# Retention recurrence with a Mish feed-forward block: mask tables and pad zeros made later, and a planner told the load times that were seen

## The chip, the core and the metric

The kernel runs on one core of a Trainium2 chip. The metric is the device time of one execution in microseconds (us). Times quoted as "the median" are medians over several executions of the same kernel. A profile records one execution; its span is a little shorter than the device time (227.4 us beside about 229 us here).

The engines are named as in the profile: PE is TensorE's matmul side, PEld its weight loads, DVE is VectorE, ACT is ScalarE, POOL is GpSimd, SP is SyncE. SPq is the instruction queue of SyncE, from which this kernel issues nearly all its DMA transfers.

## The reference, cut to what matters

```python
# B, H, S, D = 4, 8, 768, 64 ; x: 3072 x 512 ; w_in: 512 x 2048 ; w_out: 2048 x 512
gamma = 1.0 - 2.0 ** (-5.0 - np.arange(H))
state = 0
for t in range(S):
    state = gamma * state + k[:, :, t]^T v[:, :, t]        # one 64 x 64 state per batch and head
    y[:, :, t] = q[:, :, t] @ state / sqrt(D)
x = y.transpose(0, 2, 1, 3).reshape(B * S, H * D)
h = x @ w_in
g = h * tanh(softplus(h))                                  # Mish
return g @ w_out
```

## The kernel before

The recurrence is done in chunks of 128 tokens. Within a chunk the scores q k^T are masked and multiplied with v. Across chunks a state is carried, which is updated by a product k^T v (tile `u_ps`). Twelve groups of 256 tokens, g0 to g11, go through the recurrence, and the 256 output rows of each group then go through the up-projection (`h_ps`), Mish (`gt`) and the down-projection (`o_ps`). Groups 0, 1 and 2 turn their k and q on TensorE. From group 3 on, that is done by two DMA transposes (`kt`, `qt`).

The order of all instructions on all engines is fixed in advance by a small list scheduler. Each task has a modelled duration per engine, a priority and its dependencies. The planner plays the tasks through with these durations and then emits the instructions in the order of the planned starts. A duration given to the planner costs no time on the chip. It changes only the order of the queues.

```python
class Plan:
    LAT = {"PE": 0.25, "DVE": 0.1, "ACT": 0.1, "POOL": 0.12, "DMA": 2.0}
    ...
    def run(self):
        ...
        starts = {"PE": 0.9, "DVE": 0.7, "ACT": 0.7, "POOL": 0.5, "DMA": 1.3}
        ...
                d = got.eng[e]                       # the modelled duration
                order.append((now, seq, got.fn, e, d))
    ...
order, end = plan.run()
for start, seq, fn, e, d in order:                   # emitted in the planned order
    fn(e)
```

The loads of a group, the casts (copies into a 16-bit format) and products that wait for them, and the two transposes are these. Group g+1's loads are planned when its buffers come free, and all of these DMA instructions are in SyncE's one queue.

```python
# loads of group g: q in one piece, k and v in two chunks each, all issued by SyncE
loads[g, n, c] = add({"DMA": 1.4 if n == "q" else 1.18}, fn, dprio(), ...)

# k product of group g (fk), and v cast into the padded tile vpad (fv); GpSimd alone, k from group 3 on and v from group 2 on
kd = add(two(512 * n, g < DT), fk, pr, [loads[g, "k", c] for c in cs] + [tabs, open_t], ...)
vd = add(... {"POOL": 0.55 * n}, fv, pr, [loads[g, "v", c] for c in cs] + ..., ...)

def dma_transpose(g):                                # SyncE, g >= 3
    a = add({"DMA": 2.3}, fk, dprio(), [kdep[g, 0]], [], [grp[g]])     # kt, needs the k product
    b = add({"DMA": 2.3}, fq, dprio(), qdep[g], [], [grp[g]])          # qt, needs the q product

# the state update of one head pair, on TensorE: needs the k product and the v cast
def um(e):
    u = loc["u"] = psp.tile([P, len(us), P], FP32, tag="u_ps", name="u_ps")
    for i, c in enumerate(us):
        nc.tensor.matmul(u[:, i], G["k16"][:, c, hs(hp)], G["vp"][:, c * HP + hp, 0:3:2], ...)
u1 = add({"PE": mm * len(us)}, um, pr, [kdep[g, 0], vdep[g, 0]], [ub], [grp[g]])
```

The parts that the change takes hold of are the zeros of the query pads (`pq`), the eight mask tables, and the modelled durations of the loads:

```python
        def pq(e, i=i):
            ENG[e].memset(qpads[i][0:64, :, :, 1], 0.0)
            ENG[e].memset(qpads[i][64:128, :, :, 0], 0.0)
        ...
        a = add({"POOL": 2.0}, pq, (40, (i + 1) % 3))

    mks = []
    for h in range(H):
        def mk(e, h=h):
            ENG[e].tensor_scalar(
                msk[:, h], tri, float(gamma[h] ** (-C)), None, op0=ALU.mult)
        mks.append(add({"DVE": 0.35}, mk, (30,), [tabs]))
```

The masks are read from group 2 on only. Groups 0 and 1 (the "early" groups, GE = 2) use another form of the mask.

## Time and profile before

| what | value | view |
| --- | --- | --- |
| median of 3 runs | 228.63 us (228.51 to 229.49) | times |
| profiled span | 227.4 us | page |
| TensorE busy | 207.0 us, 91% | page, engine table |
| TensorE's first matmul | 9.00 us | timeline |
| TensorE idle from 9.00 to 52 us | 6.2 us | windows |
| group 2's first up-projection | 52.06 us | timeline |
| last w_out block cast begins (it waited for the landing) | 49.50 us | timeline |

These are the first lines of the page of before. The engine table gives busy time, share of the span and instruction count. The other two lines divide the span into 40 slices, each digit being tenths of busy time.

```profile
span 227.4 us, 4200 instructions
...
PE 207.0 (91%) x1688; PEld 148.3 (65%) x1688; DVE 103.4 (45%) x247; ACT 98.7 (43%) x177; POOL 71.4 (31%) x64
...
PE   0389879699999999999999899999999999999993
...
DMA  6999999999999999898999999931002011022212
```

The reader sees a TensorE that is nearly full from the ninth slice on, and a DMA that is busy until slice 26 (about 148 us) and then almost idle.

The start, from the timeline of before (start, duration, engine, line, operation, tiles, shapes; in brackets the idle time before it and what ended it):

```profile
5.24 1.04 POOL L361 TENSOR_TENSOR qpn_95<-raw_q,tab 128x512 f16<-128x512 f32 x1
5.40 2.95 DVE L283 TENSOR_SCALAR msk<-idtri 128x128 f32<-128x128 f16 x4 [3.29 <-DMA idtri<-rn_identtri]
...
8.27 0.67 DVE L361 TENSOR_TENSOR qpn_95<-raw_q,tab 128x512 f16<-128x512 f32 x1
...
9.00 1.03 PE L497 MATMUL tq<-idtri,qpn_95 128*128 128x128 f16 x8 [9.00 <-DVE qpn_95 L361]
```

Four mask products stand ahead of VectorE's half of the query product, so TensorE starts at 9.00 us.

The middle, from the windows view of before (window, its length, busy us and instruction count of PE, PEld, DVE, ACT and POOL, granted clock, DMA share, GB/s):

```profile
40.00:52.00 12.00, 9.84 (x76) 6.17 (x76) 5.81 (x12) 6.81 (x18) 4.91 (x5) 1.00 1.00 317
52.00:90.00 38.00, 38.00 (x332) 29.09 (x330) 21.65 (x56) 18.58 (x33) 19.90 (x14) 1.00 1.11 217
90.00:120.00 30.00, 29.29 (x277) 23.66 (x275) 17.31 (x49) 18.38 (x33) 15.11 (x12) 1.00 0.98 194
120.00:160.00 40.00, 39.10 (x347) 29.30 (x346) 23.69 (x61) 18.94 (x36) 16.95 (x12) 1.00 0.90 168
```

TensorE has no idle time from 52 to 90 us, 0.7 us from 90 to 120 and 0.9 us from 120 to 160. First SyncE's queue in before, from the timeline of that engine (an entry lasts while the queue is occupied with issuing, not until the data lands):

```profile
90.77 1.23 SPq L441 DMA_TRANSPOSE kt<-k_1024  x1
92.05 0.57 SPq L314 DMA_DIRECT2D raw_q<-in_q_dram  x1
92.68 2.03 SPq L322 DMA_DIRECT2D raw_k<-in_k_dram  x2
94.75 3.89 SPq L322 DMA_DIRECT2D raw_v<-in_v_dram  x2
98.82 2.00 SPq L446 DMA_TRANSPOSE qt<-q_1216  x1
102.09 1.23 SPq L441 DMA_TRANSPOSE kt<-k_1214  x1
```

Then GpSimd in the same stretch of before, the lines of the k product and the v cast:

```profile
88.84 1.90 POOL L386 TENSOR_TENSOR k_1024<-raw_k,tab 128x1024 f16<-128x1024 f32 x1 [1.43 <-PE s_ps L478]
90.68 1.04 POOL L201 CAST vpad_97<-raw_v 128x1024 f16<-128x1024 f32 x1
...
100.17 1.90 POOL L386 TENSOR_TENSOR k_1214<-raw_k,tab 128x1024 f16<-128x1024 f32 x1 [1.64 <-DMA raw_k<-in_k_dram]
102.10 1.04 POOL L201 CAST vpad_98<-raw_v 128x1024 f16<-128x1024 f32 x1
```

And the chain of work that ended last in before, in order of time (start, duration, what), cut to its waiting pieces:

```profile
93.33 6.67 DMA raw_k<-in_k_dram
...
100.17 1.86 POOL k_1214 L386
...
102.10 1.05 POOL vpad_98 L201
103.19 0.27 PE u_ps L672 x2
...
107.62 6.29 DMA raw_v<-in_v_dram
...
114.06 1.05 POOL vpad_99 L201
115.15 0.22 PE u_ps L672
...
125.39 1.05 POOL vpad_97 L201
126.47 0.27 PE u_ps L672 x2
```

There is a loop in these lines. The transpose of one group's k is issued 0.03 us after that group's k product ends (88.84 + 1.90 = 90.74). The loads of the next group stand behind it in the same queue. They are issued from 92.05 us on, and the k load lands about 100.0 us. The next k product then runs from 100.17 to 102.07, and its transpose is issued at 102.09. This period is 102.09 − 90.77 = 11.32 us (the four from 78.49 to 123.71 us last 10.3 to 12.3, 11.3 in the mean): 1.23 for issuing the transpose, 0.57 for q, 0.61 for the first half of k, 6.67 from the issue of the second half to its landing, 1.90 for the product, and 0.34 in small gaps. The v cast follows at once and takes 1.04 us, and TensorE's first state update of the group follows the cast by 0.05 us. At groups 8 and 9 TensorE had been idle for 0.48 and 0.90 us before it.

### The profile page before, as it was taken

What the parts mean: (1) busy time and instruction counts of PE and PEld (TensorE: products, weight loads), DVE (VectorE), ACT (ScalarE), POOL (GpSimd) and SP (SyncE); (2) the same over time, 40 slices, a digit from 0 to 9 for tenths busy, and PEclk for the clock granted to TensorE, in tenths of its full rate; (3) what the DMA queues carried; (4) which work ended last, traced back from release to release, by engine and by line L of the source; (5) the groups of instructions that cost most, each with busy time, mean ns of one, the idle gap of its engine ahead of it and who ended that gap; (6) DMA issues with size and microseconds to landing.
All of it is one profiled execution on the core that took longest, in us unless ns stands there. A gap on an engine that the chain in (4) does not pass through costs nothing.

```text
span 227.4 us, 4200 instructions
## 1 busy us (share of the span) xinstructions
PE 207.0 (91%) x1688; PEld 148.3 (65%) x1688; DVE 103.4 (45%) x247; ACT 98.7 (43%) x177; POOL 71.4 (31%) x64
## 2 busy tenths in 40 slices
PE   0389879699999999999999899999999999999993
PEld 0278768546857979797968668757857767444441
DVE  2978446362768472567643585747101011112221
ACT  2268666743424656566655636533613534100000
POOL 8770001518372727373636471720000000000000
PEclk9999999999999999999999999999999999999998
DMA  6999999999999999898999999931002011022212
GB/s 159 238 238 349 346 223 286 393 272 204 255 200 213 203 193 228 188 184 185 213 208 164 241 220 189 205 95 60 34 3 92 0 49 46 0 92 93 95 46 92
DMA packets 91572, 38.63 MB, mean 170 GB/s; under 512 B 69921, under 2 KB 86433, under 8 KB 91553
## 3 DMA queue, kind: packets, MB, share of 16 engines
q1 hardware_dynamic: 91264, 38.28, 74.9%
q8 instruction: 13, 0.21, 0.4%
q10 hardware_dynamic: 288, 0.09, 0.2%
q14 instruction: 7, 0.05, 0.1%
HBM read 27.35 MB, written 6.29 MB: 148 GB/s over the span
## 4 chain that ended last, share of the span: by engine, by line
PE 68%; DMA 18%; POOL 4%; DVE 3%; ACT 3%; issue 1%; SPq 1%; ACTq 0%; POOLq 0%
PE o_ps L758 33%; PE h_ps L736 25%; DMA wst<-in_moe_w_out_dram 6%; DMA wst<-in_moe_w_in_dram 4%; PE s_ps L478 3%; DMA raw_k<-in_k_dram 3%; PE y_ps L699 3%; DMA raw_v<-in_v_dram 3%; DMA idtri<-rn_identtri 2%; PE u_ps L672 1%; ACT win_90 L199 1%; PE y_ps L703 1%; PE tq L497 1%; DVE msk L283 1%; POOL vpad_97 L201 1%
## 5 line engine op out<-in xcount | busy, mean ns | idle before, releaser
L736 PE MATMUL h_ps<-xt,win_90 128*128 128x256 f16 x768 | 94.1, 273 | 2.0 <-ACT gt L741 2.0
L758 PE MATMUL o_ps<-wout_91,gt 128*128 128x512 f16 x384 | 90.4, 379 | 2.2 <-POOL wout_91 L201 1.9
L736 PEld LDWEIGHTS <-win_90 128*128 128x128 f16 x768 | 73.8, 98 | 14.7 <-issue 1.5
L741 ACT ACTIVATE gt<-h_ps 128x512 f16<-128x512 f32 x96 | 56.9, 597 | 58.2 <-PE h_ps L736 58.2
L758 PEld LDWEIGHTS <-gt 128*128 128x128 f16 x384 | 36.8, 98 | 37.9 <-issue 2.8
L769 DVE COPY osb<-o_ps 128x512 f32<-128x512 f32 x24 | 16.6, 691 | 58.5 <-PE o_ps L758 58.3
L649 DVE TENSOR_TENSOR am<-s_ps,msk 128x512 f16<-128x512 f32 x40 | 27.7, 692 | 32.1 <-PE s_ps L478 31.7
L199 ACT CAST xt<-y_ps 128x256 f16<-128x256 f32 x44 | 19.6, 446 | 21.6 <-PE y_ps L703 20.2
L201 POOL CAST vpad_99<-raw_v 128x1024 f16<-128x1024 f32 x4 | 4.2, 1038 | 20.3 <-DMA raw_v<-in_v_dram 20.3
L497 PE MATMUL tq<-idtri,qpn_95 128*128 128x128 f16 x16 | 2.1, 312 | 9.0 <-DVE qpn_95 L361 9.0
L478 PEld LDWEIGHTS <-kt 128*128 128x128 f16 x96 | 8.0, 99 | 2.6 <-issue 0.8
L497 PEld LDWEIGHTS <-qpn_95 128*128 128x128 f16 x16 | 1.7, 146 | 9.1 <-DVE qpn_95 L361 9.0
L699 PE MATMUL y_ps<-am,vpad_99 128*128 128x128 f16 x64 | 7.1, 219 | 0.0
L478 PE MATMUL s_ps<-qpad_92,kt 128*128 128x256 f16 x32 | 6.5, 288 | 0.4 <-ACT qpad_92 L199 0.4
L699 PEld LDWEIGHTS <-vpad_99 128*128 128x128 f16 x64 | 5.5, 98 | 1.7 <-DVE am L649 0.7
L683 DVE SCALAR_TENSOR_TENSOR st_1_101<-st_0_100,tab,u_ps 64x64 f16<-64x64 f16 x20 | 5.6, 279 | 2.2 <-PE u_ps L672 1.8
L478 PE MATMUL s_ps<-qpad_94,kt 128*128 128x256 f16 x32 | 6.1, 273 | 0.0
L478 PE MATMUL s_ps<-qpad_93,kt 128*128 128x256 f16 x32 | 6.1, 273 | 0.0
L536 DVE TENSOR_TENSOR am<-s_ps,idtri 128x512 f16<-128x512 f32 x8 | 5.5, 686 | 1.3 <-PE s_ps L478 1.3
L199 ACT CAST win_90<-wst 128x1024 f16<-128x1024 f32 x5 | 5.1, 1047 | 2.1 <-DMA wst<-in_moe_w_in_dram 2.1
L201 POOL CAST wout_91<-wst 128x1024 f16<-128x1024 f32 x4 | 4.2, 1042 | 5.6 <-DMA wst<-in_moe_w_out_dram 5.6
L683 DVE SCALAR_TENSOR_TENSOR st_2_102<-st_1_101,tab,u_ps 64x64 f16<-64x64 f16 x16 | 4.5, 280 | 3.1 <-PE u_ps L672 2.8
(164 smaller groups left out, 218.2 us busy)
## 6 DMA issues: line engine op xcount, KB each, us to landing
raw_q<-in_q_dram SPq DMA_DIRECT2D x12, 512.0 KB, 4.9
raw_k<-in_k_dram SPq DMA_DIRECT2D x24, 256.0 KB, 5.6
raw_v<-in_v_dram SPq DMA_DIRECT2D x24, 256.0 KB, 5.2
out_dram<-osb SPq DMA_DIRECT2D x24, 256.0 KB, 2.0
wst<-in_moe_w_in_dram SPq DMA_DIRECT2D x8, 512.0 KB, 7.6
wst<-in_moe_w_out_dram SPq DMA_DIRECT2D x8, 512.0 KB, 7.8
idtri<-rn_identtri ACTq DMA_DIRECT2D x1, 64.0 KB, 4.2
tab<-rn_tab ACTq DMA_DIRECT2D x1, 22.0 KB, 2.5
```

Source lines behind the costliest of these rows:

```text
L199: nc.scalar.copy(dst, src)
L201: ENG[e].tensor_copy(dst, src)
L478: nc.tensor.matmul(t, G["kt"][:, c, hp], G["qp"][:, :, hp, :, c * (C // 2):(c + 1) * (C // 2)].rearrange("p e y i -> p y e i"), start=True ...
L497: nc.tensor.transpose(t[:, e2, x, hh], G["qn"][:, e2 * HP + 2 * j + x, hh:hh + 2], ident)
L536: nc.vector.tensor_tensor(am, loc["s"].rearrange("p x y i -> p (x y) i"), tri.unsqueeze(1).broadcast_to((P, 4, C)), op=ALU.mult)
L649: nc.vector.tensor_tensor(am, loc["s"], msk[:, hs(hp)].unsqueeze(1).broadcast_to((P, CG, 2, C)), op=ALU.mult)
L683: nc.vector.scalar_tensor_tensor(tn[o, o], prev[o, o], tab[o, GC + hp:GC + hp + 1], loc["u"][o, i, o], op0=ALU.mult, op1=ALU.add)
L699: nc.tensor.matmul(y[:, c], G["vp"][:, c * HP + hp, hh:hh + 2], loc["am"][:, c, hh], start=(hh == 0), stop=(st is None and hh == 1))
L736: nc.tensor.matmul(h[:, j], win16[:, bp, fb * P:(fb + 1) * P], xtt[i][:, bp], start=(bp == 0), stop=(bp == NBP - 1))
L741: nc.scalar.activation(gtt[i][:, 2 * a:2 * a + 2], loc["h"], AF.Mish, scale=inv_boost)
L758: nc.tensor.matmul(ott[i, t], gtt[i][:, fb, t * P:(t + 1) * P], wout16[:, fb], start=(fb == 0), stop=(fb == NFB - 1))
L769: nc.vector.tensor_copy(osb, ott[i, t])
```

## The change

The intent was, by its description, to make the mask tables and the zeros of the late query pads once the first group is through, and to set the load model of the planner to the rates that had been seen. The diff, with comments and two neutral lines cut:

```diff
-    LAT = {"PE": 0.25, "DVE": 0.1, "ACT": 0.1, "POOL": 0.12, "DMA": 2.0}
+    LAT = {"PE": 0.25, "DVE": 0.1, "ACT": 0.1, "POOL": 0.12, "DMA": 1.5}
...
-        for d in deps:
+        for d in filter(None, deps):
...
-        starts = {"PE": 0.9, "DVE": 0.7, "ACT": 0.7, "POOL": 0.5, "DMA": 1.3}
+        starts = {"PE": 0.9, "DVE": 0.7, "ACT": 0.7, "POOL": 0.5, "DMA": 2.5}
...
-    tabs = add({"ACT": 1.6}, lambda e: None, (0,), [c_tab])
+    tabs = add({"ACT": 3.2}, lambda e: None, (0,), [c_tab])
...
-        a = add({"POOL": 2.0}, pq, (40, (i + 1) % 3))
+        a = None if i < GE else add({"POOL": 2.0}, pq, (40,))
...
-    mks = []
-    for h in range(H):
-        def mk(e, h=h):
-            ENG[e].tensor_scalar(
-                msk[:, h], tri, float(gamma[h] ** (-C)), None, op0=ALU.mult)
-        mks.append(add({"DVE": 0.35}, mk, (30,), [tabs]))
...
-            loads[g, n, c] = add({"DMA": 1.4 if n == "q" else 1.18}, fn, dprio(), [],
+            loads[g, n, c] = add({"DMA": 1.5 if n == "q" else 1.2}, fn, dprio(), [],
...
-        ld = add({"DMA": 1.3}, fn, dprio(), [], [wbuf[kind, j]])
+        ld = add({"DMA": 1.5 if kind == "in" else 1.3}, fn, dprio(), [], [wbuf[kind, j]])
...
             if g == GE - 1:
+                for h in range(H):
+                    def mk(e, h=h):
+                        if e == "ACT":
+                            nc.scalar.mul(msk[:, h], tri, float(gamma[h] ** (-C)))
+                        else:
+                            nc.vector.tensor_scalar(
+                                msk[:, h], tri, float(gamma[h] ** (-C)), None,
+                                op0=ALU.mult)
+                    mks.append(add({"DVE": 0.35, "ACT": 0.3}, mk, (17,), xdone[0]))
```

So the change has three parts: the masks move from the head of VectorE's queue to a later place on VectorE or ScalarE; the zeros of two of the three query pads, four memsets on GpSimd, go away (the early groups write these pads whole); and six constants of the planner change, which may reorder every queue and hand a task to another engine.

More of the change, by code (lines that the diff above doesn't have):

```diff
@@ L427, in load_w @@
                             [ld], [], [wbuf[kind, j]])
+    mks = []
     state = [None] * HP
```

## The prediction

> **What bounds the kernel now.** TensorE: the engine table gives it 207.0 of 227.4 us. Its 20.4 us of idleness, from the windows view, are 9.0 us before its first matmul, 6.2 between 9 and 52 us, 1.6 between 90 and 160, and 3.6 of tail. After 52 us matmuls run nearly back to back, so the time is set by when that dense stretch begins, plus later holes.
>
> Start: the first transposes wait 9.0 us for the second half of the query product on VectorE. That half begins at 8.27, behind four mask products that held VectorE from 5.40 to 8.35 (the timeline). The first took 1.85 us, the shortest 0.22.
>
> Then the load queue. By the windows it moves about 217 GB/s for the k and v loads (256-byte rows), 349 for w_in and 390 for w_out, without a break from 3 to 49 us. The last w_out block lands at about 49.5 us; the first up-projection of group 2, where the dense stretch begins, is at 52.06.
>
> **What the change does.** By the instruction order, the eight mask products leave the start of VectorE's queue (four go to ScalarE; four later on VectorE). Four memsets of query pads, 0.94 to 0.98 us each, leave GpSimd; it takes a k product, v casts and three w_in casts. Load order up to the last w_out block is unchanged; TensorE has the same instructions in another order.
>
> **Costs.** The query product's halves can start when raw_q lands, about 5.2 us. The Trainium skill, "SBUF — State Buffer", "SBUF: two separate sides", says that a VectorE operation with two SBUF inputs and a GpSimd operation reading SBUF exclude each other; the 1.85 us mask beside GpSimd's product (5.24 to 6.28) agrees. So I serialize the halves: 5.2 + 1.04 + 0.67 = 6.9 us. TensorE starts 2.1 us earlier (1.8 to 2.7).
>
> Little of that is on the path that ends last. Work before 52 us needs loads: group 1's last v at 16.8, w_in until 30.1, w_out until 49.5, and these stay. The skill, "DMA: Bandwidth & Descriptors", "Specifications", puts the line-rate limit at 512-byte transfers; the rates above agree, and no transfer grows. TensorE will idle more between its start and 52 us: about 7.3 us for 6.2. The order of down-projection parts does help: before, six down matmuls and four y groups stood between the last w_out cast and group 2's up-projection; now only two. That cast moves to GpSimd (1.04 instead of 0.69 us): 49.5 + 1.04 + 0.5 = 51.1 us, a gain of 1.0. Later holes may change by 0.5 us.
>
> **Prediction:** 227.4 us, 80% range 225.6 to 229.0. Faster by over 2%: 0.04; within 2%: 0.92; slower by over 2%: 0.04.
>
> **What would show it.** Right: first matmul near 6.9; last w_out block within 1 us of 49.5; group 2's first up-projection near 51; idleness between TensorE's start and 52 us grows, on w_out and w_in casts. Wrong: that landing moves earlier by over 2 us (late casts had starved the queue); or holes after 52 us change by over 1.5 us, since an output store now precedes a v load, and a k transpose a q transpose, in SyncE's queue.
>
> **What would make it wrong.** A queue that fills better once GpSimd casts w_in at once (dip to 165 to 189 GB/s at 32 to 34 us): up to 1.5 us more gain. A new stall in the in-order queues: up to 2 us lost.

## The result and the profile after

Four executions of the changed kernel had a median of 226.45 us (225.60 to 226.99), beside 228.68 us (228.51 to 229.49) for four of the kernel before. The ratio is 0.9892, with a 95% interval of 0.9853 to 0.9931. A gain of 1.1% is "the same" at the 2% mark, and 226.45 lies in the predicted range. It is about 1 us under the central value.

The profiled run was the slowest of the four, 226.99 us, with a span of 225.2 us. Its granted clock fell to 0.76 between 13 and 20 us, and the mean for the whole run was 0.989.

The first lines of the page of after:

```profile
span 225.2 us, 4187 instructions
...
PE 209.0 (93%) x1688; PEld 149.1 (66%) x1688; DVE 103.0 (46%) x249; ACT 95.4 (42%) x174; POOL 68.9 (31%) x61
...
PE   0868999999998999999999999999999999999993
```

TensorE is busy for 8 tenths of the second slice, where it was busy for 3 before, but the next two slices have 6 and 8 tenths, where they had 8 and 9. Its work is the same 1688 matmuls.

The start, from the timeline of after:

```profile
5.22 0.69 DVE L355 TENSOR_TENSOR qpn_95<-raw_q,tab 128x512 f16<-128x512 f32 x1 [3.10 <-DMA raw_q<-in_q_dram]
5.26 1.55 POOL L355 TENSOR_TENSOR qpn_95<-raw_q,tab 128x512 f16<-128x512 f32 x1
5.97 0.60 PE L493 MATMUL tq<-idtri,qpn_95 128*128 128x128 f16 x4 [5.97 <-DVE qpn_95 L355]
...
6.87 0.60 PE L493 MATMUL tq<-idtri,qpn_95 128*128 128x128 f16 x4 [0.29 <-POOL qpn_95 L355]
```

TensorE now starts at 5.97 us, because four of the first eight transposes need only VectorE's half of the query product. GpSimd's half took 1.55 us here, against 1.04 us before when it ran beside a mask product. That agrees with the Trainium skill, "SBUF — State Buffer", "SBUF: two separate sides", where a VectorE operation with two SBUF inputs and a GpSimd operation that reads SBUF hold the shared ports in turn: the GpSimd operation began last and took 0.51 us longer, which fits a standstill for most of the 0.65 us that the two overlapped.

The middle, from the windows view of after:

```profile
40.00:52.00 12.00, 11.28 (x82) 6.26 (x80) 6.90 (x17) 5.99 (x12) 4.99 (x4) 1.00 1.11 330
52.00:90.00 38.00, 37.06 (x312) 27.25 (x310) 22.56 (x58) 16.55 (x30) 15.91 (x11) 1.00 1.01 212
90.00:120.00 30.00, 29.49 (x283) 24.12 (x282) 17.85 (x50) 18.55 (x34) 14.30 (x10) 1.00 0.99 200
120.00:160.00 40.00, 39.62 (x362) 30.93 (x360) 23.57 (x61) 20.76 (x38) 17.65 (x12) 1.00 0.91 166
```

From 40 to 52 us TensorE is busier by 1.4 us. Then it loses 0.9 us between 52 and 90 us, where before lost none. From 90 to 160 us it loses 0.9 us instead of 1.6. So the early gain is partly given back at once, and that speaks against a plain reading of "starts earlier, ends earlier".

The chain that ended last in after, cut to its waiting pieces:

```profile
112.24 1.91 POOL k_1410 L380
...
114.17 1.23 SPq L437
...
119.78 4.91 DMA raw_v<-in_v_dram
...
124.83 1.05 POOL vpad_97 L201
...
131.38 6.36 DMA raw_v<-in_v_dram
...
137.88 1.05 POOL vpad_98 L201
...
138.97 0.27 PE u_ps L668 x2
```

The chain still runs through a k product, SyncE's queue, a load and a v cast, but in this run it meets TensorE at group 10 (138.97 us), not at group 9. Following group by group shows more than the chain does. Group 8's first state update waited too, until 116.09 us, while group 9's was ready 1.35 us before TensorE came to it.

### The profile page after: what moved, and what is told of

Read it like the earlier page. It is cut to its first block, busy times and chain, and to the rows that moved or that the text cites. A ratio compares the mean times of both kernels' runs of the same rounds, so it can differ in the third digit from the quotient of the medians.

```text
span 225.2 us, 4187 instructions
## 1 busy us (share of the span) xinstructions
PE 209.0 (93%) x1688; PEld 149.1 (66%) x1688; DVE 103.0 (46%) x249; ACT 95.4 (42%) x174; POOL 68.9 (31%) x61
## 4 chain that ended last, share of the span: by engine, by line
PE 67%; DMA 14%; SPq 10%; POOL 3%; DVE 2%; ACT 1%; issue 1%; POOLq 0%; DVEq 0%
PE o_ps L754 33%; PE h_ps L732 24%; SPq L316 7%; DMA raw_v<-in_v_dram 5%; DMA wst<-in_moe_w_out_dram 4%; DMA raw_k<-in_k_dram 3%; PE y_ps L695 3%; PE s_ps L474 3%; DMA raw_q<-in_q_dram 3%; PE u_ps L668 1%; SPq L308 1%; PE y_ps L699 1%; SPq L437 1%; POOL vpad_98 L201 1%; POOL k_1410 L380 1%
## 5 line engine op out<-in xcount | busy, mean ns | idle before, releaser
L199 ACT CAST xt<-y_ps 128x256 f16<-128x256 f32 x42 | 18.7, 445 | 20.1 <-PE y_ps L699 15.2
L201 POOL CAST vpad_98<-raw_v 128x1024 f16<-128x1024 f32 (+1 forms) x5 | 4.3, 867 | 5.8 <-DMA raw_v<-in_v_dram 3.4
L679 DVE SCALAR_TENSOR_TENSOR st_1_101<-st_0_100,tab,u_ps 64x64 f16<-64x64 f16 x20 | 5.6, 278 | 0.7 <-PE u_ps L668 0.3
L201 POOL CAST wout_91<-wst 128x1024 f16<-128x1024 f32 x3 | 3.1, 1042 | 8.6 <-DMA wst<-in_moe_w_out_dram 8.6
L679 DVE SCALAR_TENSOR_TENSOR st_1_104<-st_0_103,tab,u_ps 64x64 f16<-64x64 f16 x20 | 5.6, 278 | 0.4
L679 DVE SCALAR_TENSOR_TENSOR st_2_102<-st_1_101,tab,u_ps 64x64 f16<-64x64 f16 x16 | 4.5, 280 | 2.5 <-PE u_ps L668 2.2
```

The costliest lines, as they stand in the source:

```text
L199: nc.scalar.copy(dst, src)
L201: ENG[e].tensor_copy(dst, src)
L679: nc.vector.scalar_tensor_tensor(tn[o, o], prev[o, o], tab[o, GC + hp:GC + hp + 1], loc["u"][o, i, o], op0=ALU.mult, op1=ALU.add)
```

## The theories

**Pace.** TensorE's queue is in order. Each group's first state update has a fixed amount of TensorE work queued ahead of it. If TensorE gets there before that group's v cast, it waits, and everything that was gained before is lost at that point. The end of the kernel is then the time of the last such v cast, plus the work still queued behind it, plus about 4 us of tail and small holes. The casts come at the pace of the loads, one group per 11.3 us or so. What the new planner constants do is put more feed-forward work ahead of each group's state update, so less is left behind.

**Rivals.** (a) The prediction's own: the time is set by when the dense stretch near 52 us begins, through the start, the last w_out block and the order of the down-projection parts. (b) The early start: masks and pads out of the way are the gain. (c) The mask tables on ScalarE and the missing memsets free the engines later on.

The amount of work ahead of a group's first state update was worked out from the built kernels: the order of TensorE's instructions, with durations read from the chain of before (8 up-projection matmuls 0.87 us, 4 down-projection matmuls 0.86, a 128x128 matmul 0.0545, a 128x256 score matmul 0.109). These are estimates of TensorE time in us. The whole work is 200.9 us (200.5 with the durations as rounded here). Counted again in the traces, every entry below agrees to 0.3 us. The columns are the kernels, including those of the experiments:

| group | before, masks and pads moved only | after, constants only | q, k, v constants only | faster loads modelled | slower loads modelled |
| --- | --- | --- | --- | --- | --- |
| g4 | 48.2 | 51.6 | 49.9 | 46.5 | 51.6 |
| g6 | 71.4 | 74.9 | 73.1 | 68.8 | 75.7 |
| g8 | 93.8 | 96.4 | 95.5 | 90.4 | 99.0 |
| g9 | 104.0 | 107.5 | 106.6 | 99.7 | 110.1 |
| g10 | 115.2 | 118.6 | 117.8 | 110.8 | 121.2 |

The theory can be checked on before: the last wait is at group 9, whose cast ended at 126.42 us. 126.47 + (200.9 − 104.0) + 4.0 = 227.4 us, the span. The 4.0 is the remainder here. If the theory holds, it must be about the same in every kernel, whichever group is the last pinned one. It is: 4.1 in e1 (group 8), 3.9 in e4 (group 10), 4.0 in e10 (group 9), 4.0 in e11 (group 10) and 4.3 in e12 (group 4), each worked out in the same way from the two tables of this document.

## The experiments

Twelve kernels were run, all correct, each in five rounds beside the kernel before on the same chip. "Pinned" means that a group's first state update began 0.05 us after its v cast ended, so that the cast released it. The wait can be too short to show: the profile has no idle time of TensorE at the last pinned product of e6 and of e11.

| run | median us | before | ratio (95%) | span | first matmul | last pinned group: product begins, left behind it |
| --- | --- | --- | --- | --- | --- | --- |
| e1_after_again | 226.68 | 229.32 | 0.9900 (0.9866 to 0.9935) | 224.6 | 6.13 | g8: 116.03, 108.60 |
| e2_masks_late | 229.31 | 229.32 | 1.0007 (0.9975 to 1.0040) | 227.4 | 5.88 | g9: 126.53, 100.90 |
| e3_late_wst7 | 228.97 | 229.32 | 0.9994 (0.9964 to 1.0024) | 228.4 | 6.07 | g9: 127.49, 100.90 |
| e4_masks_head | 226.48 | 229.32 | 0.9888 (0.9859 to 0.9917) | 224.8 | 7.49 | g10: 138.60, 86.24 |
| e5_model_only | 226.19 | 228.87 | 0.9871 (0.9833 to 0.9910) | 224.2 | 6.38 | g8: 115.61, 108.60 |
| e6_masks_pads_only | 228.41 | 228.87 | 0.9982 (0.9941 to 1.0022) | 226.4 | 5.96 | g9: 125.48, 100.90 |
| e7_order_by_hand | 229.91 | 228.87 | 1.0037 (0.9993 to 1.0080) | 228.4 | 9.15 | g9: 127.50, 100.92 |
| e8_order_by_hand_masks_late | 229.34 | 228.87 | 1.0007 (0.9964 to 1.0050) | 227.4 | 5.90 | g9: 126.53, 100.91 |
| e9_plan_start_lat | 227.82 | 229.43 | 0.9932 (0.9909 to 0.9955) | 225.5 | 6.37 | g9: 124.63, 100.92 |
| e10_plan_qkv | 226.87 | 229.43 | 0.9908 (0.9873 to 0.9942) | 225.1 | 9.03 | g9: 126.83, 98.30 |
| e11_plan_fast | 232.08 | 229.43 | 1.0124 (1.0100 to 1.0147) | 230.2 | 8.33 | g10: 136.14, 94.07 |
| e12_after_slow | 225.10 | 229.43 | 0.9824 (0.9796 to 0.9851) | 223.9 | 6.01 | g4: 70.33, 153.57 |

### e1_after_again: the changed kernel once more

No edit. It ran on another chip, to have the change measured in the rounds of e2 to e4.

> The changed kernel, unaltered, as the yardstick of the runs beside it. Expected 225.6 to 227.0 us; last w_out block lands near 48.2 us, group 2's first up-projection begins near 49.8, as in its first profile.

Measured: 0.9900, so the gain is real and repeats. The profile of this run shows the last wait at group 8. From the timeline of e1, TensorE:

```profile
116.03 0.22 PE L668 MATMUL u_ps<-vpad,k 128*128 128x128 f16 x1 [0.74 <-POOL vpad L201]
```

Group 8's cast came 0.9 us later than in before (115.98 instead of 115.10). Only 108.60 us were left behind the product instead of 112.24, of which 2.6 (96.4 − 93.8) is work that now stands ahead, 0.9 is the hole at group 9, which is gone, and 0.1 is not accounted for. 0.9 − 3.64 is the whole difference of spans, −2.8 us.

### e2_masks_late: the early start alone

The order of before on every engine, except that the eight mask products are issued just ahead of VectorE's product of q for group 2. Nothing else moves, because the planner still plans them at the old place.

```diff
-    mks = []
+    mks, late = [], []
     for h in range(H):
         def mk(e, h=h):
-            ENG[e].tensor_scalar(
-                msk[:, h], tri, float(gamma[h] ** (-C)), None, op0=ALU.mult)
+            late.append(h)
...
             def fq(e):
+                while late:
+                    h = late.pop(0)
+                    nc.vector.tensor_scalar(
+                        msk[:, h], tri, float(gamma[h] ** (-C)), None, op0=ALU.mult)
                 ENG[e].tensor_tensor(
```

> The kernel before, every instruction in its old order, but the eight mask products issued just before VectorE's query product of group 2 instead of at the head of its queue. TensorE should start at 6.0 to 6.9 us. Theory LOADS (the dense stretch begins when the last w_out block is in; a start 3 us earlier is spent waiting): that block lands within 0.7 us of 49.5, group 2's first up-projection begins within 0.9 us of 52.06, and the time is 227.5 to 228.6. Rival START (the earlier start carries through): dense stretch 2 to 3 us earlier, time 225.7 to 226.7.

Measured: TensorE starts at 5.88 us, 3.1 us sooner, and the time is the same (1.0007). Rival (b) falls. The timelines of e2, first GpSimd, then TensorE, at group 9:

```profile
125.44 1.04 POOL L201 CAST vpad<-raw_v 128x1024 f16<-128x1024 f32 x1 [1.43 <-DMA raw_v<-in_v_dram]
```

```profile
126.53 0.27 PE L675 MATMUL u_ps<-vpad,k 128*128 128x128 f16 x2 [1.36 <-POOL vpad L201]
```

The same product in the timeline of before, TensorE:

```profile
126.47 0.27 PE L672 MATMUL u_ps<-vpad_97,k_1591 128*128 128x128 f16 x2 [0.90 <-POOL vpad_97 L201]
```

The wait at this product grew from 0.90 to 1.36 us. It starts at 126.53 instead of 126.47. A TensorE that comes earlier waits longer, and goes on at the same time. The line of GpSimd in e2 also corrects a reading of before: there, the profile puts the wait of this cast down to a TensorE instruction (y_ps at line 703). In before the v load had landed only at 125.24 us, 0.15 before the cast began (in e2 the two are 0.14 apart), so it was the load there too. The median, 229.31 us, lies over the written 227.5 to 228.6, but so does that of before in this call, 229.32; the ratio is what counts.

### e3_late_wst7: one more buffer for weights

As e2, and with seven staging buffers for weights instead of six, to let the load queue fill better. To make room, the mask tables are kept in half precision.

```diff
-    wst = ctx.enter_context(tc.tile_pool(name="rn_wst", bufs=6))
+    wst = ctx.enter_context(tc.tile_pool(name="rn_wst", bufs=7))
...
-    msk = cpool.tile([P, H, C], FP32)
+    msk = cpool.tile([P, H, C], FP16)
```

> As e2, with seven staging buffers for weight blocks instead of six (the mask table is held in 16 bits to make room); same order on every engine. Theory STARVED (part of what made w_out land earlier is that loads waited for a staging buffer less): SyncE no longer waits for the first w_in cast near 18 to 20.8 us, the last w_out block lands 0.8 to 1.5 us earlier than in e2, and the time falls by 0.5 to 1.3 us against e2. Rival SATURATED (the load queue was full all along): landing and time within 0.3 us of e2.

Measured: 0.9994, and the last w_out cast is at 48.78 us instead of 49.09 in e2, where the theory STARVED had written a landing 0.8 to 1.5 us earlier. The planner's own count of six slots was left as it was, so this tests the hardware's buffer and not a new order. A starved weight queue is not what bounds the kernel.

### e4_masks_head: the changed kernel with masks at the head again

As after, and four mask products are computed once more at the head of VectorE's queue, so that TensorE starts late. The order of all else is that of after.

```diff
+                    if e == "DVE" and g == 0:
+                        for h in range(4):
+                            nc.vector.tensor_scalar(
+                                msk[:, h], tri, float(gamma[h] ** (-C)), None,
+                                op0=ALU.mult)
                     ENG[e].tensor_tensor(
```

> The changed kernel, same order, with four of its mask products also computed at the head of VectorE's queue (they are computed again later, so results are unchanged). TensorE should start at about 9.0 us instead of 6.0. Theory LOADS: the last w_out block lands within 0.4 us of e1, group 2's first up-projection is at most 0.8 us later, and the time is at most 0.8 us over e1. Rival START: 2 to 3 us over e1.

Measured: TensorE starts at 7.49 us, not at the 9.0 that I had expected, since the four masks took 1.40 us together here. So the delay was 1.5 us instead of 3. It cost nothing: 0.9888 beside 0.9900 for e1. The last w_out block landed 0.56 us later than in e1 (at most 0.4 had been written) and group 2's first up-projection began 0.58 us later, which cost nothing either. Together with e2, the start is free of cost in both directions.

### e5_model_only and e6_masks_pads_only: the two halves of the change

e5 is before with only the planner's constants of the change. e6 is before with only the moved masks and the missing pad zeros, and the old constants. (The edits are the corresponding lines of the diff above.)

> The kernel before with only the planner's load constants of the change (masks and pad memsets stay where they were). Theory ORDER (the gain comes from the order in which the planner, given slower loads, queues the work: the first down-projection no longer stands ahead of up-projections and attention in TensorE's queue while its weights are still loading): 226.0 to 227.3 us, a ratio of 0.988 to 0.994, with no wait of TensorE on a w_out cast over 0.5 us. Rival UNLOADING (the gain comes from taking the masks and memsets off VectorE and GpSimd): 228 to 229.5, ratio 0.997 to 1.003.

> The kernel before with the masks and pad memsets moved as in the change, and the planner's old load constants. Theory ORDER: the 1.9 us wait of TensorE on the second w_out cast stays, ratio 0.996 to 1.002, although TensorE starts near 6 us. Rival UNLOADING: ratio 0.988 to 0.994.

Measured: 0.9871 for the constants alone, 0.9982 for the moved masks and pads (an interval that holds 1). The whole gain is that of the constants, which take no work off the chip. Rival (c) is ruled out as the cause. For rival (b) e5 alone would not do, since the new constants also put most of the masks behind the query product and TensorE starts at 6.38 us there. But e6 starts at 5.96 us without such a gain, and e10 below at 9.03 us with one.

Two details were missed. For e6 I had written that the wait of 1.9 us on the second w_out cast stays: it fell to 0.5 us, and group 2's first up-projection began at 50.68 us instead of 52.06, without a gain clear of noise. And e5 lies just under the written 0.988 to 0.994. The pins agree: e5 has the work ahead of after and ends 108.60 us after group 8's product, to the hundredth as e1; e6 has the work ahead of before and ends 100.90 us after group 9's product, as e2.

### e7_order_by_hand and e8_order_by_hand_masks_late: the order of the down-projection parts alone

This is the term that the prediction counted on. e7 is before, with only two blocks of TensorE's queue moved by hand, so that no down-projection should stand in the way of group 2's up-projection for a w_out block. e8 is e7 with the late masks of e2.

```diff
+            parts[i, t, part] = mmf
...
     order, end = plan.run()
+
+    def move(what, behind=None, before=None):
+        x = next(r for r in order if r[2] is parts[what])
+        order.remove(x)
+        n = next(n for n, r in enumerate(order) if r[2] is parts[behind or before])
+        order.insert(n + 1 if behind else n, x)
+    move((0, 0, 0), before=(0, 0, 1))
+    move((0, 1, 2), before=(0, 0, 3))
```

> The kernel before, with two moves by hand in TensorE's queue only, all other engines in their old order: the first four down matmuls go behind two blocks of up-projection (16 matmuls) and an attention unit, and the four that need no late weights (tile 1, part 2) go ahead of the eight-matmul tail that waits for the last w_out block. Theory ORDER: the wait of 1.9 us on the second w_out cast goes, group 2's first up-projection begins at 50.6 to 51.2 instead of 52.06, ratio 0.993 to 0.997. Rival LOADS ONLY (the last w_out landing sets the time, and only an earlier landing helps): ratio 0.998 to 1.002.

> As e7, with the mask products also moved away from the head of VectorE's queue, so that TensorE starts near 6 us. Theory ORDER with a bound from the last w_out block: at most 0.5 us better than e7, because the last w_out landing (about 49.3) plus cast and two matmuls is what is left. Rival START: 1.5 to 3 us better than e7, once the order no longer hides it.

Measured: 1.0037 and 1.0007. For e7 I had expected 0.993 to 0.997, and that was a miss. The wait of the down-projection for w_out on GpSimd, 1.9 us in before, is gone from the list of waits, but group 2's first up-projection began only at 51.72 us, not at the written 50.6 to 51.2. In place of that wait stands this line (from the waits of TensorE in e7: what waited for what, us in total, times, longest):

```profile
PE u_ps L672 <- POOL vpad L201: 2.8, 5, 1.1
```

The same waits in before:

```profile
PE u_ps L672 <- POOL vpad_97 L201: 1.1, 2, 0.9
PE u_ps L672 <- POOL vpad_99 L201: 0.5, 1, 0.5
```

A hole was closed and others opened downstream. They are not all due to an earlier TensorE: in the profile of e7, group 9's cast also ended 1.0 us later than in before (127.45 instead of 126.42), for a reason that stays open. In e8, where the up-projection began at 51.26 us, 0.8 us earlier than in before, the time is still that of before. (By the medians e8 is 0.57 us under e7, where at most 0.5 had been written; the intervals overlap.) Both speak against the prediction's view that the time is set near 52 us.

### e9, e10: which constants

e9 is before with only the start of the DMA (2.5), its latency (1.5) and the tables (3.2) of the change. e10 is before with only the load durations of q (1.5) and of k and v (1.2).

```diff
# e9
-    LAT = {..., "DMA": 2.0}
+    LAT = {..., "DMA": 1.5}
-        starts = {..., "DMA": 1.3}
+        starts = {..., "DMA": 2.5}
-    tabs = add({"ACT": 1.6}, ...)
+    tabs = add({"ACT": 3.2}, ...)
# e10
-            loads[g, n, c] = add({"DMA": 1.4 if n == "q" else 1.18}, ...
+            loads[g, n, c] = add({"DMA": 1.5 if n == "q" else 1.2}, ...
```

> The kernel before with three of the planner's new constants only: loads start at 2.5, landing latency 1.5, tables ready after 3.2. Theory PACE (TensorE reaches the first state-update product of a group at the pace of the v casts, which the load queue sets; the end is that moment plus the TensorE work queued behind it; the constants matter only where they change how much work is queued ahead of those products): the work ahead of groups 4 to 11 is exactly that of before (104.0 us ahead of group 9 by unit costs), so nothing changes: ratio 0.996 to 1.003; product of group 9 without slack after its cast, 100.9 us before the end. Rival ANY NEW ORDER (every re-planning with the new start or latency helps): 0.988 to 0.994.

> The kernel before with only the planner's durations of q, k and v loads raised (1.4 to 1.5 and 1.18 to 1.2). Theory PACE: 95.5 us of work stand ahead of group 8's product (before 93.8) and 106.6 ahead of group 9's (before 104.0); with casts done at 115.2 to 116 and 125.5 to 126.5 us the span is 224.5 to 225.7, a ratio of 0.988 to 0.994; group 9's product begins over 0.5 us after its cast. Rival: the gain needs the w_in constant or the earlier start; ratio 0.997 to 1.003.

Measured for e10: 0.9908, a span of 225.1, inside what I had written. Two constants changed by 0.1 and 0.02 us give most of the gain, by putting 2.6 us more work ahead of group 9's product. I had also written that this product would begin over 0.5 us after its cast. It was pinned, so that detail was wrong. e10 is also the clearest evidence against rivals (a) and (b): its TensorE starts at 9.03 us and its group 2 begins the up-projection at 51.98 us, both as in before (9.00 and 52.06), and it is faster all the same. The sixth constant, that of w_in, was not run alone.

Measured for e9: 0.9932, where I had expected 0.996 to 1.003. That is a miss, and it taught something. From the timeline of e9, TensorE:

```profile
124.63 0.27 PE L672 MATMUL u_ps<-vpad,k 128*128 128x128 f16 x2 [0.26 <-POOL vpad L201]
```

The work left behind the product is as in before, 100.92 us. But the cast of group 9 ended 1.85 us earlier (124.57 instead of 126.42). So e9 gained through the other term of the same sum, earlier casts rather than more work ahead. SyncE's queue in e9 has output stores at slightly different places. That this is why the casts came earlier is argued only, and stays open. Between kernels with the same TensorE work ahead of groups 4 to 11, the cast of group 9 was seen at 124.57 (e9), 125.43 (e6), and 126.42 to 127.45 (before, e2, e3, e7, e8), with one profile each.

### e11_plan_fast and e12_after_slow: the planner told wrongly, in both directions

e11 is before with loads modelled faster than before had them (q 1.3, k and v 1.1, w_in 1.2). e12 is after with loads modelled slower than after has them.

```diff
# e11, from before
-            loads[g, n, c] = add({"DMA": 1.4 if n == "q" else 1.18}, ...
+            loads[g, n, c] = add({"DMA": 1.3 if n == "q" else 1.1}, ...
-        ld = add({"DMA": 1.3}, ...
+        ld = add({"DMA": 1.2 if kind == "in" else 1.3}, ...
# e12, from after
-            loads[g, n, c] = add({"DMA": 1.5 if n == "q" else 1.2}, ...
+            loads[g, n, c] = add({"DMA": 1.6 if n == "q" else 1.25}, ...
```

> The kernel before with the planner told that loads are faster than they are (q 1.3, k and v 1.1, w_in 1.2). Theory PACE: only 99.7 us of work stand ahead of group 9's product (before 104.0), so TensorE reaches it early, waits for the cast at about 126.5 us all the same, and has 105.2 us left: span 230.5 to 232.5, ratio 1.012 to 1.023. Rival PREFIX (the time is set by when group 2's up-projection begins, near 52 us): within 0.5% of before.

> The changed kernel with the planner's q, k and v durations raised once more (1.6 and 1.25): 99.0, 110.1 and 121.2 us of work ahead of groups 8, 9 and 10 (changed kernel 96.4, 107.5, 118.6), 51.6 ahead of group 4 as in the changed kernel. Theory PACE: the waits at groups 8 and 10 go, group 4's at about 70 us stays and is the last one, 153.7 us before the end; span 223.4 to 224.3, ratio to before 0.983 to 0.988, so 0.2 to 0.6% faster than the changed kernel. Rival: TensorE is bound by its work there; ratio as the changed kernel, 0.988 to 0.992, or loads come later because buffers are freed later.

Measured for e11: 1.0124, slower, although its TensorE starts earlier than that of before (8.33 us) and its group 2 begins the up-projection earlier too (51.21 instead of 52.06). Rival (a) cannot explain that. Pace does: every group from g5 to g10 is pinned, and 105.42 us are left behind group 9's product (105.2 had been written ahead of the run). The span, 230.2 us, is just under the written 230.5 to 232.5, because group 9's cast ended at 124.74 us and not at the 126.5 that had been assumed. From the timeline of e11, TensorE at group 9:

```profile
124.79 0.27 PE L672 MATMUL u_ps<-vpad,k 128*128 128x128 f16 x2 [0.57 <-POOL vpad L201]
```

This product begins 1.68 us earlier than in before and the kernel ends 2.8 us later, because 4.5 us more are left behind it, of which 4.3 (104.0 − 99.7) are work.

Measured for e12: 225.10 us and 0.9824, just below the written 0.983 to 0.988, which its interval overlaps. The span, 223.9 us, is inside the written 223.4 to 224.3, and 153.57 us are left behind group 4's product (153.7 had been written). It beats both kernels. Its only pinned group is g4. The one line of this kind among the waits of TensorE in e12:

```profile
PE u_ps L668 <- POOL vpad L201: 0.8, 1, 0.8
```

From group 8 on, the casts are 0.9 to 2.4 us ahead of TensorE, and TensorE has no idle time at all from 90 to 160 us (30.00 of 30 and 40.00 of 40 us in the windows view). e12 was compared with after only through the kernel before, on different chips: 0.9824 beside 0.9892 and 0.9900. The intervals of e12 and e1 do not overlap (0.9796 to 0.9851, and 0.9866 to 0.9935).

A small sum suggests why the constants act as they do. In the planner's model, one group of loads and transposes takes q + 4 × (k or v) + 2 × 2.3 us. That is 10.72 us in before, 10.90 in after, 11.20 in e12 and 10.30 in e11. The chip takes about 11.3 (the period above). Output stores, 0.75 us each in the model, are left out on the planner's side. The planner lets TensorE reach a group when its model says that the group will be there. Where it believes in faster loads than the chip has, TensorE comes too soon at every group, and the error would add up from group to group. This is argued from the sum and not shown by a run of its own.

One limit of these runs: new constants re-plan all engines, and no run moved TensorE's feed-forward work alone. What speaks for pace is that the remainder of the sum stays within 3.9 to 4.3 us whichever group is pinned last, and that the spans of e10 and e12 were written down ahead of the runs.

## Why the prediction was right, and where it was not

The time and the class were right. The reasons were right in part only.

- **"The time is set by when that dense stretch begins, plus later holes."** This step failed. In e2, e8 and e11 that stretch began earlier than in before (51.65, 51.26 and 51.21 us instead of 52.06), and the spans were 227.4, 227.4 and 230.2, beside 227.4. In e10 it began at 51.98 us and the span was 225.1. The time is set by the last pinned state update between group 4 and group 10. The prediction had read the holes after 52 us (1.6 us from 90 to 160) as small change. They were small in us, but each is a point where TensorE is put back to the clock of the loads, which wipes out whatever had been gained ahead.
- **"Later holes may change by 0.5 us."** By size this held: the holes from 52 to 160 us sum to 1.6 us in before, 1.8 in after and 1.3 in e1. What failed is that the prediction added them to a start time. The sum that fits has other terms: of the 2.8 us of span between before and e1, 2.6 are work moved ahead of group 8 and 0.9 a hole gone at group 9, less a cast that came 0.9 later. No term of the prediction stood for work moved ahead of a wait.
- **"The order of down-projection parts does help … a gain of 1.0."** Done alone in e7, and with an earlier start in e8, it gained nothing (1.0037 and 1.0007).
- **"Little of that is on the path that ends last" (the start).** Right, and shown in both directions (e2 and e4). But the prediction's reason was the w_out loads until 49.5 us. In e2, what little of the earlier start was left at 52 us (0.4 us) was waited away at group 9.
- **First matmul near 6.9 us.** It came at 5.97, and the second four transposes at 6.87. The serialization that the estimate rested on is in the trace (1.55 us instead of 1.04); that the first four transposes need only one half was overlooked.
- **Last w_out block within 1 us of 49.5.** Its cast began at 48.21, so it landed 1.3 us earlier, just outside.
- **Group 2's first up-projection near 51.** It was at 49.79.
- **Idleness from the start to 52 us grows from 6.2 to 7.3.** It did not grow. The profile of after has 4.8 us (46.03 us from 5.97 to 52, of which TensorE was busy 41.21), but at a granted clock of 0.96 in that stretch. e1, at 1.00, has 6.0 us (45.87 from 6.13 to 52, busy 39.92).
- **The size.** Predicted gain 1.2 us, measured 2.2 by the medians. The two are close by luck: a gain of 1.0 from the order of the down-projection parts, which does not exist, stood in for one of 2 that had been left out.
- **"The load queue bounds the early part", with 217 GB/s for 256-byte rows.** The rates hold in both profiles (217 and 212 GB/s from 52 to 90 us; the Trainium skill, "DMA: Bandwidth & Descriptors", "Specifications", has 512 bytes as the least for full rate, and w_in and w_out with longer rows moved 349 and 393 GB/s in slices of the page of before, 349 and 384 in that of after). What was missing is that the same slow k and v loads also clock TensorE later, through SyncE's queue.

The Trainium skill, "Perfetto Trace Analysis", "Optimization Strategy", advises finding the gaps on the engine in question and the instruction that each waits for. Followed literally for the gaps of 0.5 to 1 us before `u_ps`, it would have led to the v casts and the loads at once. I had sorted gaps by size and stopped at the two big ones.

**What stays open.** Why the v casts come 1 to 2 us apart in kernels with the same TensorE work ahead of them was not settled. How much of the 11.3 us is the queue's order and how much is the DMA engines' own time was not tested either. In the DMA view of before from 84 to 104 us, in 40 slices of 0.5 us, the busy tenths are:

```profile
DMA  9999999999994800997369999999993999956039
```

The engines are mostly full, with pauses at 91 to 92 us and near 102 to 103.5 us, when SyncE has waited for the k product and is issuing its transpose. By this line some 2 to 3 us of this period are idle. Issuing a group's loads ahead of the previous group's transposes would attack them. It is the next thing that I would try, and it was not run.

## What to carry to other kernels

Here an in-order engine met a producer again and again, and its end was the producer's last late delivery plus the work queued behind that point. So look for the last wait, however short, and ask how much work stands behind it, and don't count a gain ahead of it. A schedule made from a model should not be told shorter durations than the chip shows for the resource that really paces it: with longer ones it puts more other work ahead of the wait (a loss of 1.2% with loads told too fast, a gain of 1.8% with loads told slowest, which includes the moved masks, 0.2% at most by the centre of e6, all with the same matmuls). By the sum above even the slowest setting, 11.20 us a group, stayed under the chip's 11.3, so what happens beyond that was not tried. Test a change that consists of moves and of new planner constants in halves, since the constants alone may reorder every queue.

## What the Trainium skill lacked or had wrong

- "Perfetto Trace Analysis", "DMA Instruction — HWDGE (DVE, Sync)", says that the issuing sequencer waits for the semaphores itself and is free for the next instruction only when it has issued. The trace agrees (the transpose was issued 0.03 us after the k product, and the next load 0.05 us after the transpose's issue ended). The page does not draw the consequence, that loads queued behind a waiting transpose are held back as well. Here that closes a loop of 11.3 us per group in the mean of four.
- "Perfetto Trace Analysis", "Optimization Strategy", says that a gap which repeats can mean too few buffers. Here the repeated gap before `u_ps` (three to five times in before, e2 and e7, 0.2 to 1.4 us) was changed by the planner's constants alone (three waits totalling 1.6 us in before, one of 0.5 in e10). A further staging buffer for weights did nothing (e3, 0.9994); further buffers for q, k and v were not tried.
- No page that I read says how short waits of an in-order queue that a producer paces are to be valued: 3.1 us of earlier start were worth nothing (e2), and 2.6 us of work moved ahead of one wait gave 1%.
- "SBUF — State Buffer", "SBUF: two separate sides", has the later of the two operations wait until the earlier one is done. The direction is confirmed: 1.55 us instead of 1.04 for the GpSimd product when VectorE's two-input product had begun 0.04 us sooner. The size is nearly so: 0.51 us lost of 0.65 us of overlap, with durations on GpSimd that the profile gives only roughly.
